# An expert layer behind attention: rows scattered to their experts' places and loaded as plain stretches, the gate kept in the table, and the first two network steps in one fixed order

## The chip, the core and the metric

One core of a Trainium2 chip runs the whole kernel in one launch. Its engines work beside each other, each in the order of its own queue: TensorE (PE; its weight loads are listed as PEld), VectorE (DVE), ScalarE (ACT), GpSimd (POOL) and SyncE (SP), which here only issues DMAs. The metric is the time of one execution on the device in microseconds, the median of the runs. The profile is that of one such execution.

## The reference

Three layers, one behind the other; r, k and v are [4, 8, 768, 48].

```python
for t in range(768):                       # attention with a decaying state
    y[:, :, t] = r_t @ (state + (u * k_t) v_t^T)
    state = w * state + k_t v_t^T
x = y as [3072 tokens, 384]
h = x @ w_in                               # [384, 2048]
x = (h - tanh(h)) @ w_out                  # [2048, 384]
logits = normalized(x) @ normalized(expert_emb).T / tau      # 8 experts
e = argmax(logits); gate = softmax(logits)[e]
out[token] = gate * (relu(x[token] @ w1[e]) @ w2[e])         # w1 [8, 384, 1024], w2 [8, 1024, 384]
```

Each token goes to one expert, so the rows have to be sorted by expert on the device before the last layer.

## The kernel before

Tokens are worked in 24 attention tiles of 128 and in 8 blocks of 384 (TB = 3 tiles). Every product of the two networks is three matmuls, since each factor is held as a high and a low part (`hi`, `lo`; `ghi`, `glo`).

**Start.** Up to line 1276 the order is written by hand (`tc.manual_schedule`): the first three attention tiles, the conversion of the first weights (`convert`, L255 to L261 on VectorE, then `split`, L268 on ScalarE and L269 on GpSimd) and their attention states. Behind `startup.close()` (L1277) a planner with a timeline model orders the instructions of each engine; `tc.issue_after(x)` is a lower bound that the program sets for it. The steps of the first network come from the loop at L1340: one step is `ffn1` (nine matmuls into `ph`, L547), `squares` (L599, L600), `small_tanh` (L608 to L615) and, some steps later, `ffn2` (nine matmuls into `acc`, L562). Steps 0 and 1 belong to this planned part, so do the state products of the first tiles (L466, added to the state by L477) and the conversions behind the first. `IDLE` puts fillers (L538) ahead of some steps; `fill` writes them to a bank that the step overwrites. All accumulators are PSUM tiles of one pool of eight banks.

**Attention of later tiles** (`attn_tile`, L489) runs ahead of the network by about a block: GpSimd does the decays (L346, L349), the bonus (`rk`, L383, L384, two buffers under the tag "xr") and the masks (`am`, L402); VectorE puts the scores into them (L419); then TensorE multiplies (L445).

**Routing** (`finish`, L636) is a generator with a stop after each part, one per block: ScalarE copies the rows out of PSUM (`xr`, L651, two buffers), SyncE stores them to `xs` in the order of the tokens (L653); VectorE finds the best expert as a one-hot matrix (`oh`, L666), TensorE counts with it (`pk`, L671), VectorE casts each token's place (`irow`, L686); GpSimd scatters the token numbers to `tab` at those places (L697); norms, exponent and gate follow, and SyncE stores the gate behind the row in `xs` (L720).

**Experts.** They are worked in an order found on the device. `order_first` (L736) runs one block ahead of the end and names the first two. For each expert `places` (L810) reads its piece of the table (`gts`), `rows` (L818) gathers its rows from `xs` by an indirect DMA on GpSimd (L798), three tiles of 128 and, for the first three experts, a fourth that is called the overflow tile here; `load_expert` (L828) loads and converts its weights (L840, L843, L851, L852); `wide` (L894) turns the rows (`columns`, L874 to L878) and does eight steps (L547, relu L629 and L631, L562); `put` (L881) scales by the gate (L883) and scatters to `out` (L803). For the first expert the three tiles are gathered, turned and its first step multiplied while the last block is still in the first network (`COL0`); its fourth tile has to wait for the last block's routing (L1458 to L1462).

Of the kernel before, what the change touches and what calls it, by code (L numbers as in the profile page):

```python
# [29 lines left out]
def rwkv__then__tanh_ffn__then__top1_moe_kernel(  # L30
# [46 lines left out]
    NEARLY = 1  # L77
    NNAR = 2
    COL0 = (13, 15)
# [3 lines left out]
    ISTORE = 14  # L83
    FA = 6
# [6 lines left out]
    lastg = None  # L91
# [8 lines left out]
    xs = dram.tile([NT, RW], F32, name="xs")  # L100
    xd = dram.tile([NT, 2 * DM], F32, name="xd")
# [134 lines left out]
    def convert(t, dst_hi, dst_lo, win_chunk=False, by_f=False):  # L236
# [13 lines left out]
        def ops():  # L250

            for l, h in cuts:
                x = ps.tile([P, 512], I32, tag="p", name="bits")
                x = x[:, :TOK].rearrange("p (k d) -> p k d", d=P) if by_f else x[:, :l.shape[1]]
                nc.vector.tensor_scalar(out=x, in0=h, scalar1=3, scalar2=0x3FFFFFFF,  # L255
                                        op0=ALU.logical_shift_left, op1=ALU.bitwise_and)
                yield
                nc.vector.scalar_tensor_tensor(out=x, in0=l, scalar=29, in1=x,
                                               op0=ALU.logical_shift_right, op1=ALU.bitwise_or)
                yield  # L260
                mark["cut"] = nc.vector.scalar_tensor_tensor(out=l, in0=h, scalar=-0x40000000, in1=x,  # L261
                                                             op0=ALU.bitwise_and, op1=ALU.bitwise_or).ins
                yield
# [332 lines left out]
    def squares(ph):  # L596
        z = work.tile([P, TOK], F32, name="z")
        q = work.tile([P, TOK], F32, name="q")
        nc.scalar.activation(out=z, in_=ph, func=AF.Square)  # L599
        nc.scalar.activation(out=q, in_=z, func=AF.Square, scale=SS, bias=sb_t)  # L600
        return z, q
# [34 lines left out]
    def finish(j, acc, part=None):  # L636
        l = work.tile([P, TB, E], F32, name="l")
        ssq = work.tile([P, TB], F32, name="ssq")
        gw = work.tile([P, TB, 2], F32, name="gw")
# [6 lines left out]
        for t in range(TB):  # L646
            if part is not None:
                xr = part[:, t, :DM]
            else:
                xr = work.tile([P, DM], F32, name="xr")  # L650
                nc.scalar.activation(out=xr, in_=acc[t][:, :DM], func=AF.Copy)  # L651
            n = TB * j + t
            nc.sync.dma_start(out=xs[n * P:n * P + P, :DM], in_=xr)  # L653
# [40 lines left out]
        root = None  # L694
# [841 lines left out]
```

## Time and profile before

| | |
|---|---|
| runs | 781.63, 781.47, 778.47 us; median 781.47 |
| the profiled execution | 780.2 us, of which the span from first to last instruction 778.6 |
| PE busy | 761.0 us (98%), 6157 matmuls; mean granted clock 0.991 |
| DVE, ACT, POOL busy | 481.3, 454.9, 300.5 us |
| chain that ended last, by engine | PE 87%, ACT 3%, DMA 3%, issue 3%, the rest 4% |
| DMA | 87.36 MB, mean 112 GB/s |

The page gives busy times over the whole span. With TensorE busy nearly throughout, the page itself tells little of where time can be won; the list of what each engine waited for and the table of stretches (windows) tell more. A window's row gives, for each engine, its busy time within the stretch and the number of its instructions, then TensorE's granted clock as a share of full speed, the share of the DMA engines that moved data, and the rate.

### The profile page before, as it was taken

What the parts mean: (1) busy time and instruction counts of PE and PEld (TensorE: products, weight loads), DVE (VectorE), ACT (ScalarE), POOL (GpSimd) and SP (SyncE); (2) the same over time, 40 slices, a digit from 0 to 9 for tenths busy, and PEclk for the clock granted to TensorE, in tenths of its full rate; (3) what the DMA queues carried; (4) which work ended last, traced back from release to release, by engine and by line L of the source; (5) the groups of instructions that cost most, each with busy time, mean ns of one, the idle gap of its engine ahead of it and who ended that gap; (6) DMA issues with size and microseconds to landing.
All of it is one profiled execution on the core that took longest, in us unless ns stands there. A gap on an engine that the chain in (4) does not pass through costs nothing.

```text
span 778.6 us, 16001 instructions
## 1 busy us (share of the span) xinstructions
PE 761.0 (98%) x6157; PEld 723.0 (93%) x6157; DVE 481.3 (62%) x1076; ACT 454.9 (58%) x1054; POOL 300.5 (39%) x319
## 2 busy tenths in 40 slices
PE   9899999999999999999999999999899999999996
PEld 5689899999999999999999999998889999999996
DVE  7967975786666755765755754756564445545430
ACT  5687776665656557556656666777253445544431
POOL 3743670564641750850751540132431124312311
PEclk9899999999999999999999999999999999999999
DMA  8934350344231330330232201160463345545500
GB/s 273 302 101 140 116 182 22 93 133 130 60 119 60 87 121 21 91 131 25 90 87 91 89 2 62 32 191 32 120 217 92 114 152 184 170 145 172 179 30 31
DMA packets 41831, 87.36 MB, mean 112 GB/s; under 512 B 9718, under 2 KB 21424, under 8 KB 40722
## 3 DMA queue, kind: packets, MB, share of 16 engines
q1 hardware_dynamic: 37042, 76.74, 31.3%
q0 software_dynamic: 4288, 9.51, 3.8%
q8 instruction: 50, 0.82, 0.5%
q14 instruction: 35, 0.29, 0.1%
q10 hardware_dynamic: 416, 0.00, 0.0%
HBM read 67.38 MB, written 19.40 MB: 111 GB/s over the span
## 4 chain that ended last, share of the span: by engine, by line
PE 87%; ACT 3%; issue 3%; DMA 3%; DVE 1%; SPq 1%; POOL 1%; POOLq 0%; DVEq 0%; ACTq 0%
PE acc L562 37%; PE ph L547 36%; PE py L445 5%; PE pa L414 3%; DMA eraw<-in_moe_w_dram 1%; PE pt L874 1%; DMA ktab<-xs,gts 1%; PE warm L154 1%; PE pst L466 1%; SPq L720 1%; PE ph L958 1%; PE ph L538 1%; PE accn L562 1%; ACT wq L851 1%; PE pl L294 0%
## 5 line engine op out<-in xcount | busy, mean ns | idle before, releaser
L547 PE MATMUL ph<-xt,wq 128*128 128x384 f32 (+4 forms) x1712 | 337.4, 340 | 2.1 <-ACT wt L286 1.3
L547 PEld LDWEIGHTS ph<-xt,wq 128*128 128x128 f32 x1712 | 300.5, 188 | 6.2 <-ACT wt L286 1.5
L562 PE MATMUL acc<-wq,ghi 128*128 128x392 f32 (+2 forms) x1120 | 289.0, 344 | 0.1
L562 PEld LDWEIGHTS acc<-wq,ghi 128*128 128x128 f32 (+1 forms) x1120 | 200.6, 187 | 5.0 <-issue 1.0
L562 PE MATMUL acc<-wq,glo 128*128 128x392 f32 (+2 forms) x552 | 182.7, 341 | 0.0
L599 ACT ACTIVATE z<-ph 128x384 f32<-128x384 f32 x128 | 62.6, 489 | 89.1 <-PE ph L547 88.6
L608 DVE TENSOR_TENSOR ph<-ph,z 128x384 f32<-128x384 f32 x128 | 71.8, 561 | 51.9 <-ACT z L599 51.2
L562 PEld LDWEIGHTS acc<-wq,glo 128*128 128x128 f32 (+1 forms) x552 | 103.0, 188 | 0.3
L610 ACT ACTIVATE ghi<-ph 128x384 fp32r<-128x384 f32 x128 | 62.8, 490 | 60.2 <-DVE ph L609 56.2
L615 DVE TENSOR_TENSOR glo<-ph,ghi 128x384 fp32r<-128x384 f32 x128 | 70.8, 553 | 42.6 <-ACT ghi L610 42.5
L803 POOL DMA_INDIRECT out_dram<-ob,gts x27 | 27.9, 1034 | 153.6 <-ACT ob L883 148.4
L600 ACT ACTIVATE q<-z,sb_t 128x384 f32<-128x384 f32 x128 | 78.9, 617 | 3.5
L609 DVE SCALAR_TENSOR_TENSOR ph<-q,ph 128x384 f32<-128x384 f32 x128 | 71.8, 561 | 11.8 <-ACT q L600 3.5
L612 ACT ACTIVATE mk<-z,lz_t 128x384 bf16<-128x384 f32 x128 | 77.2, 603 | 0.0
L631 DVE SCALAR_TENSOR_TENSOR glo<-ph,ghi 128x384 fp32r<-128x384 f32 (+2 forms) x56 | 30.7, 548 | 64.5 <-ACT ghi L629 64.5
L629 ACT ACTIVATE ghi<-ph 128x384 fp32r<-128x384 f32 (+4 forms) x56 | 27.4, 489 | 67.3 <-PE ph L547 67.3
L852 DVE TENSOR_TENSOR wq<-eraw,wq 128x768 fp32r<-128x768 f32 x60 | 55.3, 961 | 15.8 <-ACT wq L851 15.2
L851 ACT ACTIVATE wq<-eraw 128x768 fp32r<-128x768 f32 x64 | 50.5, 837 | 9.8 <-DMA eraw<-in_moe_w_dram 9.6
L383 POOL TENSOR_TENSOR rk<-rkv 128x384 f32<-128x384 f32 x18 | 18.4, 1021 | 91.4 <-ACT xr L651 49.6
L269 POOL TENSOR_TENSOR wq<-wraw,wq 128x768 fp32r<-128x768 f32 (+1 forms) x17 | 30.7, 1806 | 43.3 <-ACT wq L268 40.4
L402 POOL TENSOR_TENSOR am<-ident,cd 128x512 f32<-128x512 f32 x36 | 36.9, 1050 | 8.9 <-DVE cd L388 8.9
L482 POOL TENSOR_TENSOR st<-st,pw 112x384 f32<-112x384 f32 x20 | 16.7, 837 | 50.7 <-DVE st L475 35.0
(289 smaller groups left out, 897.0 us busy)
## 6 DMA issues: line engine op xcount, KB each, us to landing
eraw<-in_moe_w_dram SPq DMA_DIRECT2D x32, 768.0 KB, 4.8
rkv<-in_rows_dram SPq DMA_DIRECT2D x18, 640.0 KB, 5.7
tt<-in_cols_dram SPq DMA_DIRECT2D x22, 448.0 KB, 4.6
xd<-xt SPq DMA_DIRECT2D x8, 1152.0 KB, 6.1
wraw<-in_moe_w_in_dram SPq DMA_DIRECT2D x8, 768.0 KB, 9.0
wraw<-in_moe_w_out_dram SPq DMA_DIRECT2D x8, 768.0 KB, 9.3
xs<-xr SPq DMA_DIRECT2D x21, 192.0 KB, 2.6
rkv<-in_rows_dram SPq DMA_DIRECT2D x4, 256.0 KB, 9.8
```

The source lines that it names most:

```text
L445: nc.tensor.matmul(out=self.py[32 * g:32 * g + 32, kk, :], lhsT=lhs, rhs=rhs, start=start, stop=stop)
L547: mark["ph"] = nc.tensor.matmul(out=ph, lhsT=lhs[a][:, kk, :], rhs=rhs(b, kk), start=(kk == 0 and p == 0), stop=(kk == nk - 1 and p == 2)).ins
L562: mm = nc.tensor.matmul(out=acc[t][:lhs.shape[1]], lhsT=lhs, rhs=rhs(b, i), start=(i == span[0] and p == 0), stop=(i == span[1] - 1 and p ...
L599: nc.scalar.activation(out=z, in_=ph, func=AF.Square)
L600: nc.scalar.activation(out=q, in_=z, func=AF.Square, scale=SS, bias=sb_t)
L608: nc.vector.tensor_tensor(out=ph, in0=ph, in1=z, op=ALU.mult)
L609: nc.vector.scalar_tensor_tensor(out=ph, in0=q, scalar=KC, in1=ph, op0=ALU.add, op1=ALU.mult)
L610: mark["ghi"] = nc.scalar.activation(out=ghi, in_=ph, func=AF.Copy).ins
L612: nc.scalar.activation(out=mk, in_=z, func=AF.Relu, bias=lz_t, accum_out=zx[:, step:step + 1])
L615: mark["glo"] = nc.vector.tensor_tensor(out=glo, in0=ph, in1=ghi.bitcast(F32), op=ALU.subtract).ins
L851: nc.scalar.activation(out=hi[c][:, a], in_=t[:, a], func=AF.Copy)
L852: engs[s % len(engs)].tensor_tensor(out=lo[c][:, a], in0=t[:, a], in1=hi[c][:, a].bitcast(F32), op=ALU.subtract)
```

## The change

Six things are done.

1. Rows are no longer stored in the order of the tokens. `finish` keeps the three copies (tags "x2t", "x2t", "xr") and, once the places are known, GpSimd scatters the whole rows to a new DRAM tensor `xe` at their places.
2. The gate goes as a second word into the token's entry, and `tab` is scattered behind the gate instead of ahead of the norms. `finish` has one stop more, and `FIN` names the steps of the following block at which it goes on.
3. `rows` is a plain load of a stretch of `xe` on SyncE; `places` moves to GpSimd's queue; the weights of the next expert are issued behind the row loads.
4. `clear_rows` writes zeros to the middle of each expert's region of `xe`, so that places that no token takes hold numbers.
5. Of the first expert's steps, the first is multiplied behind the last accumulation of the first network, and the next expert is begun one step later (`NEARLY`, `COL0`).
6. The product, state and conversion work of steps 0 and 1 of the first network goes into the part with the fixed order, the state addition between the two squares; the scaling of the expert embedding goes to ScalarE and its transposes to step 2.

```diff
-    NEARLY = 1
+    NEARLY = 2
-    COL0 = (13, 15)
+    COL0 = (13,)
+    FIN = (3, 4, 6, 10)
+    xe = dram.tile([E * REG + P, DM], F32, name="xe")
...
@@ finish
-                xr = work.tile([P, DM], F32, name="xr")
+                xr = work.tile([P, DM], F32, name="xr", tag="xr" if t == TB - 1 else "x2t")
                 nc.scalar.activation(out=xr, in_=acc[t][:, :DM], func=AF.Copy)
-            nc.sync.dma_start(out=xs[n * P:n * P + P, :DM], in_=xr)
+            src.append(xr)
...
-        for t in range(TB):
-            with tc.issue_after(root) if root else ExitStack():
-                apart("tab", nc.gpsimd.indirect_dma_start(
-                    out=tab, out_offset=bass.IndirectOffsetOnAxis(ap=irow[:, t:t + 1], axis=0),
-                    in_=tokid[:, TB * j + t, :], in_offset=None))
-            if j == NB - 1 and t == 0:
-                root = norms()
+        def scattered(to, t, rows):
+            ins = nc.gpsimd.indirect_dma_start(
+                out=to, out_offset=bass.IndirectOffsetOnAxis(ap=irow[:, t:t + 1], axis=0), in_=rows, in_offset=None)
+            apart("tab" if to is tab else "xe", ins)
+            return ins.ins
+
+        yield
+        for t in range(TB):
+            mark["xe"] = scattered(xe, t, src[t])
         yield
-        if j < NB - 1:
+        with tc.issue_after(mark["xe"]):
             norms()
...
-        nc.vector.tensor_copy(out=gw, in_=se[:, :, None].to_broadcast([P, TB, 2]))
+        nc.vector.tensor_copy(out=tokid[:, own, 1:2].bitcast(F32), in_=se[:, :, None])
         for t in range(TB):
-            mark["gw"] = nc.sync.dma_start(out=xs[n * P:n * P + P, DM:], in_=gw[:, t, :]).ins
+            mark["tab"] = scattered(tab, t, tokid[:, TB * j + t, :])
@@ order_first
-        for t in flat:
-            nc.gpsimd.memset(t, 0.0)
@@ rows
-            lastg = gather(g, gts[:m, jb, t], n).ins
+            mark["rows"] = nc.sync.dma_start(out=g[:, :DM], in_=xe[bass.ds(row + t * P, m), :]).ins
@@ load_expert
-            with tc.issue_after(mark["gts"]) if jb == 1 else ExitStack():
+            with tc.issue_after(mark["rows"]) if jb > 0 else ExitStack():
@@ put
-        a = nc.scalar.activation(out=ob, in_=acc, func=AF.Copy, scale=g[:, DM:DM + 1])
+        a = nc.scalar.activation(out=ob, in_=acc, func=AF.Copy, scale=gt[:, 1:2].bitcast(F32))
@@ ahead
-        if jb > 0:
-            places(jb + 1, 0, nt)
-        nxt = rows(jb + 1, 0, nt, NT)
+        nxt = rows(jb + 1, 0, nt)
+        if jb == 0:
+            places(0, TB, TB + 1)
+        places(jb + 1, 0, nt)
@@ embedding_rows, embedding_columns
-        mark["en"] = nc.vector.tensor_scalar(out=en, in0=en, scalar1=en_n, scalar2=None, op0=ALU.mult).ins
+        with tc.issue_after(mark["act"]):
+            nc.scalar.activation(out=en, in_=en, func=AF.Copy, scale=en_n)
@@ clear_rows, called at step ISTORE behind store_x
+        regions = xe[:E * REG].rearrange("(e r) d -> e r d", e=E)[:, TOK - P:TOK + P].rearrange("e (a p) d -> a p e d", p=P)
+        with tc.issue_after(mark["w"]):
+            for a in range(2):
+                nc.sync.dma_start(out=regions[a], in_=zero[:, None, :].to_broadcast([P, E, DM]))
@@ start
     embedding_rows()
+    early = [ffn1([win(p, 0) for p in range(2)], columns_of(xts[0]), NK, TOK)]
+    a[0].state_product()
+    early.append(squares(early[0], a[0].state_add))
+    convert_now(True)
+    a[TB].decay_r(nc.vector)
+    mark["pool"] = split(*ready[2])[1]
+    early.append(ffn1([win(p, 1) for p in range(2)], columns_of(xts[0]), NK, TOK))
+    a[1].state_product()
+    a[2].turned()
+    def next_rows():
+        a[1].state_add()
+        mark["act"] = a[2].turned_rows()
+    early.append(squares(early[2], next_rows))
     startup.close()
...
@@ end of the last block
+    with tc.issue_after(mark["acc"]):
+        next(wides[0])
+    for _ in range(3):
+        next(fin)
+    sl = sl + rows(0, TB, TB + 1)
     for _ in fin:
         pass
-    places(0, TB, TB + 1)
-    places(1, 0, TB + (KOV > 1))
     order_rest()
-    sl = sl + rows(0, TB, TB + 1, NT)
```

## Rows read from the trace of the kernel before

**Rows 1.** What TensorE waited for over the span: us in total, times, longest us.

```profile
PE pt L874 <- DMA ktab<-xs,gts: 2.9, 1, 2.9
PE pk L671 <- DVE oh L666: 1.5, 1, 1.5
...
PE pa L414 <- POOL wq L269: 1.3, 1, 1.3
```

**Rows 2.** Windows round the hand-over: PE, PEld, DVE, ACT, POOL; clock, DMA, GB/s.

```profile
540.20:541.70 1.50, 0.07 (x1) 0.00 (x0) 1.36 (x9) 1.46 (x5) 0.00 (x0) 1.00 0.06 22
541.70:559.50 17.80, 17.76 (x108) 17.45 (x108) 8.72 (x52) 4.21 (x11) 7.41 (x9) 1.00 0.33 87
559.50:562.40 2.90, 0.05 (x1) 0.05 (x1) 1.14 (x2) 1.58 (x2) 2.51 (x3) 1.00 1.05 397
562.40:567.50 5.10, 5.10 (x25) 5.00 (x26) 4.79 (x12) 3.33 (x6) 0.30 (x1) 0.67 0.71 202
```

**Rows 3.** Chain that ended last, 536 to 584 us: start, us, what.

```profile
548.15 3.50 SPq L720
...
555.51 6.79 DMA ktab<-xs,gts
...
569.16 1.58 PE ph L547 x9
```

**Rows 4.** Timeline of GpSimd at the hand-over: start, us, instruction [idle before].

```profile
543.42 1.03 POOL L697 DMA_INDIRECT tab<-tokid,irow  x1 [6.74 <-DVE key L773]
...
546.96 0.96 POOL L697 DMA_INDIRECT tab<-tokid,irow  x1 [0.30 <-issue]
```

**Rows 5.** Timeline of VectorE at the hand-over.

```profile
542.97 0.17 DVE L686 CAST irow<-row 128x3 int32<-128x3 f32 x1
```

**Rows 6.** DMA issues: out<-in, queue, count, KB each, median us to landing.

```profile
xs<-xr SPq DMA_DIRECT2D x21, 192.0 KB, 2.6
```

**Rows 7.** The output's scatters, line 803, from 500 us on: ns least/median/most; landing.

```profile
L803 POOL DMA_INDIRECT out_dram<-ob,gts x27: 923/1016/1401, 575.0 to 773.5; - x27
...
DMA to landing us min/median/max: 2.5/3.0/5.9
```

**Rows 8.** Windows of the start.

```profile
21.40:27.20 5.80, 5.65 (x57) 4.58 (x57) 5.73 (x16) 2.52 (x6) 3.77 (x5) 1.00 1.05 288
27.20:30.20 3.00, 1.09 (x9) 0.97 (x8) 3.00 (x7) 2.90 (x10) 3.00 (x2) 1.00 1.03 373
30.20:37.30 7.10, 6.45 (x32) 4.72 (x33) 7.10 (x13) 6.63 (x19) 6.82 (x5) 0.56 0.85 255
```

**Rows 9.** Timeline of ScalarE at the start.

```profile
25.99 0.94 ACT L268 ACTIVATE wq<-wraw 128x768 fp32r<-128x768 f32 x1 [2.24 <-DVE wraw L261]
26.81 0.50 ACT L599 ACTIVATE z<-ph 128x384 f32<-128x384 f32 x1
27.18 0.66 ACT L477 ACTIVATE st<-pst 48x192 f32<-48x192 f32 x2
27.86 0.61 ACT L600 ACTIVATE q<-z,sb_t 128x384 f32<-128x384 f32 x1
```

**Rows 10.** Timeline of TensorE at the start.

```profile
35.74 2.08 PE L538 MATMUL ph<-ones 128*128 128x384 bf16 x6 [0.47 <-ACT ktok L360]
```

**Rows 11.** Timelines of GpSimd, VectorE and TensorE in one block of the first network.

```profile
249.84 1.02 POOL L383 TENSOR_TENSOR rk<-rkv 128x384 f32<-128x384 f32 x1 [20.15 <-DMA xs<-xr]
...
256.26 2.05 POOL L402 TENSOR_TENSOR am<-ident,cd 128x512 f32<-128x512 f32 x2
...
259.82 1.33 DVE L419 COPY_PREDICATED am<-cmask,pa 128x512 f32<-128x512 uint8 x2
...
264.43 0.42 PE L445 MATMUL py<-tt,st 112*32 112x128 f32 x8
```

**Rows 12.** Timeline of SyncE behind the start.

```profile
108.29 0.94 SPq L525 DMA_DIRECT2D xd<-xt  x2
137.03 0.34 SPq L324 DMA_DIRECT2D tt<-in_cols_dram  x1
```

More of the change, by code (lines that the diff above doesn't have):

```diff
@@ L90, in rwkv__then__tanh_ffn__then__top1_moe_kernel @@
     wides = {}
-    lastg = None
     final = None
@@ L250, in ops @@
         def ops():
[L252 to L262, printed above, removed]
+            bits = {}
+            for n, s in sorted(((n, s) for n in range(2) for s in range(3)), key=lambda x: x[::-1] if abreast else x):
+                l, h = cuts[n]
+                if s == 0:
+                    x = ps.tile([P, 512], I32, tag="p", name="bits")
+                    x = x[:, :TOK].rearrange("p (k d) -> p k d", d=P) if by_f else x[:, :l.shape[1]]
+                    bits[n] = x
+                    nc.vector.tensor_scalar(out=x, in0=h, scalar1=3, scalar2=0x3FFFFFFF,
+                                            op0=ALU.logical_shift_left, op1=ALU.bitwise_and)
+                elif s == 1:
+                    nc.vector.scalar_tensor_tensor(out=bits[n], in0=l, scalar=29, in1=bits[n],
+                                                   op0=ALU.logical_shift_right, op1=ALU.bitwise_or)
+                else:
+                    mark["cut"] = nc.vector.scalar_tensor_tensor(out=l, in0=h, scalar=-0x40000000, in1=bits[n],
+                                                                 op0=ALU.bitwise_and, op1=ALU.bitwise_or).ins
                 yield
@@ L638, in finish @@
         ssq = work.tile([P, TB], F32, name="ssq")
-        gw = work.tile([P, TB, 2], F32, name="gw")
+        src = []
         for t in range(TB):
@@ L810, in places, with rows @@
     def places(jb, t0, t1):
-        with tc.issue_after(lastg) if jb > 1 else tc.issue_after(mark["gw"]):
-            eng = nc.gpsimd if jb > 1 else nc.sync
-            row = eng.value_load(sxi[0:1, jb, 0:1], min_val=0, max_val=(E - 1) * REG)
-            mark["gts"] = eng.dma_start(out=gts[:, jb, t0:t1], in_=tab[bass.ds(row + t0 * P, (t1 - t0) * P), :]
-                                        .rearrange("(t p) b -> p t b", p=P)).ins
-    def rows(jb, t0, t1, n):
-        nonlocal lastg
+        row = nc.gpsimd.value_load(sxi[0:1, jb, 0:1], min_val=0, max_val=(E - 1) * REG)
+        nc.gpsimd.dma_start(out=gts[:, jb, t0:t1], in_=tab[bass.ds(row + t0 * P, (t1 - t0) * P), :]
+                            .rearrange("(t p) b -> p t b", p=P))
+    def rows(jb, t0, t1):
+        row = nc.sync.value_load(sxi[0:1, jb, 0:1], min_val=0, max_val=(E - 1) * REG)
         res = []
@@ L1331, in step2 @@
             accs[j] = [ps.tile([P, DL], F32, tag="p", name=f"acc{t}") for t in range(TB)]
-        ffn2(i, spans[j], g, wout, accs[j])
+        mark["acc"] = ffn2(i, spans[j], g, wout, accs[j])
     third = attention(2)
@@ L1448, in rwkv__then__tanh_ffn__then__top1_moe_kernel @@
             if j == NB - 1 and i in (8, 9, 12, 15):
-                next(ld, None)
+                with tc.issue_after(mark["ghi"]) if i == 15 else ExitStack():
+                    next(ld, None)
             if j == NB - 1 and i in COL0:
@@ L1483, in rwkv__then__tanh_ffn__then__top1_moe_kernel @@
             nc.gpsimd.dma_start(out=gt, in_=tab[bass.ds(row, P), :])
-            gather(xo[0], gt, NT)
+            nc.gpsimd.dma_start(out=xo[0][:, :DM], in_=xe[bass.ds(row, P), :])
             for _ in narrow(0, (gt, xo[0])):
```

60 lines of the change are left out of this document (28 added, 32 removed).

## The prediction

> **What bounds the kernel now.** I read the busy lines of the page first (table above): TensorE is busy 761.0 of 778.6 us, so only what stands between its instructions, and the stretches in which its clock is low, can be won. Next the list of TensorE's waits [rows 1], then the windows round the two places where they lie [rows 2, 8], then what each wait hangs on [rows 3 to 5, 9, 10]. The reader is to see that from 100 to 540 us TensorE waits for nothing, so the attention and the first network pay only if this change hurts them, and that the change touches both places that do pay.
>
> Place one is the hand-over from the first network to the experts. TensorE stands 1.46 us for the one-hot matrix of the last block, then has 17.8 us of work, then stands 2.86 us for the fourth tile of rows of the first expert, and after this second stop its granted clock is 0.67 on average for 5.1 us, part of it at 1.2 instead of 2.4 GHz [rows 1, 2]. The chain to that tile is long: SyncE writes the rows, the gate stores hold SyncE's queue for 3.50 us, the table is read, and the indirect gather takes 6.79 us from issue to use, since the first expert weights were issued just ahead of it [rows 3].
>
> Place two is the start, 21 to 37 us. VectorE is full there (5.73 of 5.80, 3.00 of 3.00, 7.10 of 7.10 us), TensorE has 1.09 us of work in the middle 3.00, and in the 7.10 us behind it its clock is 0.56 [rows 8]. ScalarE is full as well behind 27.2 (2.90 of 3.00, 6.63 of 7.10), and at 35.74 six fillers, with the third step's matmuls behind them, wait for its copy L360 [rows 8, 10].
>
> **The change, part by part.** The sum is made against the profiled execution, 780.2 us with a span of 778.6; the median of the runs is 781.47, 1.27 higher.
>
> *One product step put behind the last accumulation* (COL0, and the wide step behind mark "acc"). The nine matmuls of the first expert's first step are 1.58 us [rows 3]. Before, they ran ahead of the last accumulation; now they stand between it and the one-hot product. All before that comes 1.6 us sooner, and the 1.46 us stop is filled. VectorE gets one more relu (L631) among the routing operations, ScalarE one more copy; half a microsecond each, so I take 1.4 of 1.46, bounds 0.8 and 1.5.
>
> *The fourth tile.* Removed: three row stores, three gate stores on SyncE, the table read and the indirect gather as links of its chain. Added: three indirect scatters of whole rows to xe, then one plain load. In the old time less 1.6: the places are cast at 543.14 [rows 5], so 541.5; the first scatter goes at 541.8 and three of 1.0 with 0.3 between end at 545.7 [rows 4]. The nearest scatter of rows of this width is that of the output, 2.5, 3.0 or 5.9 us from issue to landing (least, median, most) [rows 7], so the last one, issued at 544.5, lands at 547.5, at the latest at 550.4. The load of 192 KB is bounded by the row store of the same size, 2.6 us [rows 6], and by the old gather, 6.79 [rows 3]: the tile is there at 550, with the worst of both at 557.2. TensorE, which ends the one-hot product near 540.1 and still has the 17.8 us of [rows 2], asks at 557.9. The stop of 2.86 us goes whole, with 0.7 to 8 us to spare; I go by the nearest rows, median and 2.6. I take 2.9; bounds 1.5 and 2.9, the lower if the weights collide with the load as they did before.
>
> *The clock behind it.* 5.1 us at 0.67 lose 5.1 x 0.33 = 1.7 us [rows 2]; the fall comes only behind the stop. I take 1.6, bounds 0 and 1.7. What is late next: the short stop of the overflow tile's product for L961 stays, and the conversions of the second expert's weights, which used to fall into the stop, now run beside a busy TensorE. VectorE is busy 4.79 of 5.1 us there [rows 2], but a step is used two steps later, so I count 0.3 against it, up to 1.5.
>
> *Norms, gates and table later.* The gate is needed first when an output is copied, behind all eight steps of the first expert; that work hides it, at no cost. Without that cover it would be three table scatters at 1.0 with gaps of 0.3 [rows 4], 4 us. The table is read on GpSimd's queue behind those scatters; the first output scatters queue behind the read and have the same cover.
>
> *Rows and weights of the later experts on SyncE.* TensorE does not wait there now (none of [rows 1] lies there): 0. SyncE loses 24 row and 24 gate stores.
>
> *Clearing part of xe.* Two stores on SyncE of 128 x 8 x 384 x 4 bytes, 3.1 MB together. They go on SyncE's queue behind the stores of x that are issued at 108.3; its next load is at 137.0 [rows 12]. At the 202 to 397 GB/s of [rows 2] they take 8 to 16 us. That gap hides it: 0. Without it, a load would be late by as much, and a tile of attention with it.
>
> *Row scatters in the seven earlier blocks.* Three more per block on GpSimd, 1.0 and 0.3 us each: 4.0 us. The narrowest place of the block that I followed has 4.8 us of room: GpSimd's masks end at 258.3 and the product that uses them starts at 264.4, with 1.33 us of VectorE between [rows 11]. GpSimd also loses a wait: it stood 20.15 us there for the old row stores to free a buffer [rows 11]. I take 0, bounds 0 and the rival below.
>
> *The first two steps in a fixed order.* ScalarE idled 2.24 us ahead of the conversion at 25.99, and z, the two state copies and q (0.50 + 0.66 + 0.61 = 1.77 us) came behind it [rows 9]; the first step's product that they follow stands at the head of the first window of [rows 8]. Written ahead of it, they leave a chain that is full down to 35.74: 1.8 us. The scaling of the expert rows moves from VectorE to ScalarE, as one copy: nearest is the 0.5 of [rows 9], so minus 0.5. The fillers took 2.08 us at the low clock [rows 10], half at the full one: plus 1.0. Sum 2.3. Upper bound: from 27.2 to 37.3 TensorE did 1.09 + 6.45 x 0.56 = 4.7 us of work at full clock in 10.1, so 5.4. Lower bound: VectorE is full in all three windows and loses almost nothing, so 0, and minus 2 if the new order stalls an engine that the planner had filled.
>
> On the clock there, what the rows show is single short waits, 1.3 us the longest [rows 1], and a clock of 0.56 behind them. The Trainium skill ("TensorE: Matmul & The Clock Gate", section on psum-queue depth-cycling) says that cycling through the PSUM banks makes TensorE idle in bits, often enough that the clock swings between its two levels. By that rule the fall would stay even when the longest wait is gone, and the start would be worth 1.3, not 2.3. No row decides it; the waiting for banks (L360 frees one) speaks for it, the 1.09 of 3.00 us against.
>
> Sum: 1.4 + 2.9 + 1.6 - 0.3 + 2.3 = 7.9. From 780.2 that is 772.3, from the median 773.6; I say **773.0**.
>
> **The rivals.** *Only the hand-over pays.* The start stays bound by VectorE, full in [rows 8], and its clock low: gain 5.6 to 6.6, time 774 to 776.5. For it: VectorE's windows; against: what TensorE waits for at 35.74 is a copy of ScalarE.
>
> *The wait changes its place.* The tile comes behind the weights, with the worst landing of [rows 7] and the 6.79 of [rows 3] and another 1 us, or the conversions hold the relus. Then 1.5 to 4 us of the hand-over are lost, clock and all: gain 4 to 6.4 with the start as forecast, 1.6 to 4 without: 775 to 780. Against it: 8 us of spare by the nearest rows.
>
> *Slower: GpSimd sets the pace of attention.* Its queue is in order, and a row scatter holds what stands behind it until the places are known. With 4.0 us of scatters and w us of waiting per block against 4.8 us of room, attention is late by w - 0.8, seven times. It cancels the gain at w = 0.8 + 7.9/7 = 1.9 us; at w = 3 it costs 15.4 us: 780.2 - 7.9 + 15.4 = 788. For it: the room is small. Against it: the 20 us stop that goes away, and each scatter is written two steps behind its places. Output scatters lasted 0.92 to 1.40 us each beside a working VectorE [rows 7]. The Trainium skill ("SBUF — State Buffer", section Who interferes with whom) says that a VectorE instruction in a two-port mode blocks GpSimd's descriptor writing for its whole length; by that rule more scatters mean more of the 1.40 kind, 0.4 x 3 = 1.2 us of w per block, which still falls short of 1.9.
>
> *It does not do what it says.* The planner may place the product step elsewhere, and the 1.46 us stop stays: within the second rival's range.
>
> **How the numbers follow.** Forecast (both places pay, 770.5 to 775.5): 0.53. Only the hand-over, 774 to 776.5: 0.18. The wait changes its place, 775 to 780: 0.15. The start at its upper bound, 3 us better than forecast, 769 to 771: 0.06. Slower by GpSimd: 0.05; a stalled start of minus 2 with a poor hand-over, 779 to 782: 0.03. The range leaves out the last two cases and the far end of the third: 768.5 to 778.5. A measurement of this kernel can tell about 0.5% from no change, 3.9 us. Faster by more, below 777.6: 0.53 + 0.18 + 0.04 + 0.06 = 0.81; within: 0.11 + 0.03 = 0.14; slower by more: 0.05.
>
> **What would show it.** TensorE's waits after the change: no stop over 0.5 us for the one-hot matrix or a tile of rows, and a granted clock of 1.0 for the 20 us behind. The fourth tile's load on SyncE lands near 551 in the old time. The third step's matmuls start before 36 us instead of behind the fillers of [rows 10]. No TensorE stop between 100 and 530; if one shows, the attention rival holds. The prediction fails if the load waits for the weights, or if TensorE at 25 to 40 us is as slow as before.

## The result, and the profile after

The changed kernel takes 786.71 us (median of 6 runs, 784.79 to 790.61); beside it the kernel before took 780.19 (778.47 to 781.63). The ratio is 1.009 with a 95% interval of 1.0061 to 1.0119: slower by nearly 1%, where 773.0 was forecast and 778.5 was the end of the range. The profiled execution took 787.1 us, with a span of 785.5 against 778.6.

First the list of TensorE's waits (us in total, times, longest us). Both stops of the hand-over in [rows 1] are gone, the one for the one-hot matrix and the one for the tile of rows. A longer one stands in their place (the first line below), two new ones of 2 us elsewhere, and two short ones in the last block:

```profile
PE acc L567 <- ACT ghi L636: 5.4, 1, 5.4
PE pt L289 <- ACT ktok L365: 2.1, 1, 2.1
PE pst L471 <- issue: 2.0, 5, 0.5
...
PE acc L567 <- ACT ghi L617: 0.7, 1, 0.7
PE acc L567 <- DVE glo L622: 0.5, 1, 0.5
```

Windows round the hand-over, columns as in [rows 2]: 22.3 us without a gap, then 5.4 us of nothing, then 5.9 us at a granted clock of 0.61, so most of it at 1.2 instead of 2.4 GHz.

```profile
543.40:565.70 22.30, 22.30 (x139) 21.73 (x138) 10.38 (x62) 5.95 (x16) 7.69 (x11) 1.00 0.46 98
565.70:571.10 5.40, 0.00 (x0) 0.00 (x0) 2.95 (x4) 3.57 (x6) 2.35 (x4) 0.79 0.51 168
571.10:577.00 5.90, 5.89 (x22) 5.33 (x23) 3.95 (x14) 1.81 (x5) 3.50 (x5) 0.61 0.95 280
```

What TensorE waits for is read from the timelines of GpSimd, SyncE, ScalarE and TensorE, in that order (start, us, instruction, [idle before]):

```profile
550.71 0.96 POOL L701 DMA_INDIRECT xe<-xr,irow  x1 [0.31 <-issue]
...
555.68 1.04 POOL L701 DMA_INDIRECT tab<-tokid,irow  x1 [2.71 <-DVE exc L1005]
...
568.72 5.88 POOL L814 DMA_DIRECT2D gts<-tab  x8 [9.47 <-DMA tab<-tokid,irow]
```

```profile
554.47 0.35 SPq L823 DMA_DIRECT2D ktab<-xe  x1
555.01 1.51 SPq L823 DMA_DIRECT2D rkv<-xe  x3
556.74 0.59 SPq L823 DMA_DIRECT2D u_bc<-xe  x1
557.95 1.05 SPq L839 DMA_DIRECT2D eraw<-in_moe_w_dram  x2
```

```profile
566.98 1.58 ACT L850 ACTIVATE wq<-eraw 128x768 fp32r<-128x768 f32 x2 [8.31 <-DMA eraw<-in_moe_w_dram]
569.10 1.58 ACT L850 ACTIVATE wq<-eraw 128x768 fp32r<-128x768 f32 x2 [0.54 <-DMA eraw<-in_moe_w_dram]
570.59 0.47 ACT L636 ACTIVATE ghi<-ph 128x384 fp32r<-128x384 f32 x1
```

```profile
571.11 2.29 PE L567 MATMUL acc<-wq,ghi 128*128 128x384 f32 x6 [5.41 <-ACT ghi L636]
```

SyncE's queue works in order. All row loads need the last row scatter, so it stands until 554.47; the second expert's weights are written behind five of these loads and go out at 557.95. The first of them land near 567, 9 us after their issue. ScalarE works in order too: the relu of the first expert's seventh step stands behind four conversions of these weights, and TensorE behind the relu.

The same order stood in the kernel before. Its one-hot product, its first conversions of these weights and that relu were:

```profile
541.73 0.18 PE L671 MATMUL pk<-oh,tri 128*128 128x8 bf16 x1 [1.46 <-DVE oh L666]
...
560.38 1.58 ACT L851 ACTIVATE wq<-eraw 128x768 fp32r<-128x768 f32 x2 [5.01 <-DMA eraw<-in_moe_w_dram]
...
563.97 0.47 ACT L629 ACTIVATE ghi<-ph 128x384 fp32r<-128x384 f32 x1
```

There the weights went out at 554.76 and landed 5.6 us later. The one-hot product came 3.3 us earlier too, so times are best counted from it: the weights' issue is at 13.0 us before and 12.9 after, hence not later; their landing is at 18.7 before and 22.0 after; the relu is done at 22.7 before and 26.0 after. TensorE asks for it at 20.7 in the changed kernel. Before, the stop for the tile of rows, from 17.8 to 20.6, put this asking off behind 22.7, so the wait did not show.

To see where the rest went, the span is cut at four TensorE instructions that every kernel has: the last product of the logits (pl), the one-hot product of the sixth block, that of the last block (pk), and the count after the first expert (pok). For the profiled run of after they are:

```profile
126.69 0.63 PE L299 MATMUL pl<-wt,ent 128*32 128x128 f32 x12
439.83 0.18 PE L677 MATMUL pk<-oh,tri 128*128 128x8 bf16 x1
545.02 0.18 PE L677 MATMUL pk<-oh,tri 128*128 128x8 bf16 x1
587.05 0.18 PE L1036 MATMUL pok<-ok,ones 128*128 128x8 bf16 x1
```

The differences, in us, here and in the experiments' traces (each one execution; names as below). Where the hand-over is written alike, two executions still differ by 2.6 us (before and new_start) and by 3.4 (wf_ghi and wf_ghi_again), so a smaller difference in that column is weak evidence by itself; the changed kernel's three executions lie at 42.0 to 43.0:

| kernel | to pl | to 6th pk | to last pk | to pok | to end |
|---|---|---|---|---|---|
| before | 128.97 | 307.33 | 105.43 | 38.50 | 198.4 |
| forecast change | -2.3 | 0 | -1.4 | -4.2 | 0 |
| after, as profiled | 126.69 | 313.14 | 105.19 | 42.03 | 198.4 |
| after_again | 128.89 | 307.31 | 106.27 | 42.98 | 198.4 |
| after_same | 127.13 | 312.70 | 105.86 | 41.98 | 198.3 |
| weights_first | 129.44 | 307.31 | 104.75 | 34.93 | 198.5 |
| wf_ghi | 128.82 | 307.32 | 103.71 | 35.26 | 198.4 |
| wf_ghi_again | 126.87 | 307.32 | 103.56 | 38.68 | 198.5 |
| wf_ghi_tab | 127.22 | 309.88 | 104.16 | 36.53 | 198.4 |
| weights_mid | 126.73 | 312.59 | 104.01 | 42.60 | 198.5 |
| no_tab | 126.80 | 307.32 | 105.38 | 41.18 | 198.3 |
| tab_late | 129.30 | 307.32 | 105.60 | 39.21 | 198.4 |
| tab_late_same | 128.06 | 311.20 | 105.88 | 40.45 | 198.3 |
| new_start | 130.19 | 307.50 | 105.35 | 35.94 | 198.3 |
| before_wf | 131.01 | 307.30 | 105.53 | 34.60 | 198.5 |
| product_behind | 129.48 | 307.37 | 104.97 | 36.70 | 198.4 |

So the later experts are as they were, and three stretches went otherwise than forecast: the hand-over (last pk to pok), the last block ahead of it, and, in some executions, the first block. In the profiled run they make the 6.9 us of the two spans: -2.3 at the start, +5.8 in the first block, -0.2 in the last, +3.5 in the hand-over.

### The profile page after: what moved, and what is told of

Its sections match the earlier page's. It is cut to its first block, busy times and chain, and to the rows that moved or that the text cites. A ratio compares the mean times of both kernels' runs of the same rounds, so it can differ in the third digit from the quotient of the medians.

```text
span 785.5 us, 16012 instructions
## 1 busy us (share of the span) xinstructions
PE 762.3 (97%) x6157; PEld 723.4 (92%) x6157; DVE 481.3 (61%) x1075; ACT 454.8 (58%) x1055; POOL 293.1 (37%) x312
## 4 chain that ended last, share of the span: by engine, by line
PE 84%; DMA 5%; issue 4%; ACT 2%; DVE 2%; POOL 1%; SPq 1%; POOLq 0%; DVEq 0%; ACTq 0%
PE acc L567 36%; PE ph L552 35%; PE py L450 5%; PE pa L419 3%; DMA eraw<-in_moe_w_dram 3%; PE pt L873 1%; PE pst L471 1%; DMA xe<-xr,irow 1%; DMA rkv<-xe 1%; ACT wq L850 1%; PE accn L567 1%; SPq L823 0%; POOL out_dram L804 0%; PE pt L289 0%; DVE bits L263 0%
## 5 line engine op out<-in xcount | busy, mean ns | idle before, releaser
L851 DVE TENSOR_TENSOR wq<-eraw,wq 128x768 fp32r<-128x768 f32 x60 | 54.9, 956 | 19.2 <-ACT wq L850 18.7
L701 POOL DMA_INDIRECT tab<-tokid,irow x24 | 23.8, 992 | 36.5 <-DVE tokid L726 28.8
L701 POOL DMA_INDIRECT xe<-xr,irow x21 | 20.7, 987 | 40.1 <-issue 31.2
```

Of the source, the lines that this page charges most:

```text
L701: ins = nc.gpsimd.indirect_dma_start(out=to, out_offset=bass.IndirectOffsetOnAxis(ap=irow[:, t:t + 1], axis=0), in_=rows, in_offset=None)
L851: engs[s % len(engs)].tensor_tensor(out=lo[c][:, a], in0=t[:, a], in1=hi[c][:, a].bitcast(F32), op=ALU.subtract)
```

## The experiments

Ratios are to the kernel before beside it on the same chip; its median lay between 778.8 and 780.2. Each kernel starts from the changed one unless it says otherwise.

**weights_first.** SyncE loads the second expert's first two pieces of weights ahead of all these rows.

```diff
+    ld1 = load_expert(1, sxi[0:1, 1, 1:2], gate0)   # its two first loads
+    next(ld1)
     sl = sl + rows(0, TB, TB + 1)
...
```

> The changed kernel with one move: SyncE issues the first two loads of the second expert's weights ahead of the load of the fourth tile of rows and of the second expert's rows, not behind them. Theory A (weights that come late, on a ScalarE that works in order: the loads stood on SyncE behind row loads that had to wait for the row scatters, the conversions waited 8.3 us, and the relu of the next step stood behind them): the loads go out near 545 us instead of 557.95, the conversions wait for nothing, TensorE's stop of 5.4 us and the low clock behind it go, and the kernel takes 778 to 782 us, against 786.7 of the changed kernel. Theory B (the row scatters themselves make the hand-over longer, in whatever order the loads stand): the weights now share the DMA engines with the scatters, the fourth tile lands later than its 560 us by as much as the weights gain, and the time stays at 785 us or more.

776.38 us, ratio 0.9965 (0.9948 to 0.9982): theory A, and below its 778. That is 12.5 thousandths below the changed kernel as first run and 9.3 below after_again, whose trace lacks the gaps of the last section: some 7 us for the move itself. From pk to pok it takes 34.93 us, 7.1 less than the changed kernel; the last of the two loads goes out at 540.30. What TensorE waits for from 500 to 600 us:

```profile
PE pt L975 <- ACT hh L972: 1.6, 2, 0.9
PE acc L569 <- DVE glo L624: 0.5, 1, 0.5
PE acc L569 <- ACT ghi L619: 0.3, 1, 0.3
```

**conv_behind.** The conversions stand behind the relus instead (their generator is advanced from step 6 on, `if i >= 6 if jb == 0 else ...`).

> The changed kernel with one move: the conversions of the second expert's first two pieces of weights are issued behind the relus of the first expert's last two steps, not ahead of them. The loads stay where they are, late. Theory A1 (only the order on ScalarE costs, the late weights alone would be covered): the stop of 5.4 us for the relu goes, and the time is 779 to 783 us. Theory A2 (the late weights cost wherever the conversions stand): the stop moves to the first product of the second expert, which now waits for the conversions, and the time stays within 2 us of the 786.7 of the changed kernel.

781.14 us, 1.0033 (1.0015 to 1.0052). By the time A1, by the trace A2: the 5.4 us stop is gone, but late weights now hold up what stands behind them on ScalarE and VectorE: 3.0 us for hh of the fourth tile's own product, and 2.9 of the next step for xn, a copy of that tile. Its profiled run was no faster in the hand-over (42.75 us). The order on ScalarE alone is not the cause.

**weights_mid.** The weights between the fourth tile's load and the second expert's rows.

> The changed kernel with the second expert's first two weight loads on SyncE between the fourth tile of rows and the second expert's rows: ahead of four loads (672 KB), but still behind the wait for the row scatters. It tells apart why the weights of the changed kernel landed near 569 us, 11 us after their issue. Waiting theory (the loads stand behind the scatters' end at 554.5): issue moves from 557.95 to about 555 and the landing by those 3 us only, so the relu still stands behind the conversions for 2 to 3 us: 780 to 783 us. Sharing theory (the four row loads ahead of them took the DMA engines): issue at 555, landing 5.5 us after it as in the kernel before, near 560.5, so the conversions end before the relu is due: 776 to 778 us.

785.87 us, 1.0079 (1.0059 to 1.0098): worse than both theories, with the gaps of the last section in its trace. The weights went out at 554.88, yet landed 7.6 us later, and now the rows behind them were late:

```profile
PE pt L885 <- DMA rkv<-xe: 5.6, 1, 5.6
```

Neither the place on the queue nor the four row loads explain that. The DMA queues of after do (packets, MB, share of the 16 engines' time), from 559 to 564 us and then from 564 to 569; q1 carries SyncE's loads, q0 GpSimd's scatters:

```profile
q1 hardware_dynamic: 135, 0.26, 86.1%
q0 software_dynamic: 21, 0.00, 0.4%
```

```profile
q1 hardware_dynamic: 678, 1.32, 70.5%
q0 software_dynamic: 32, 0.00, 0.5%
```

In the first stretch (5 us of 16 engines) a packet of the loads, some 2 KB, took 5 x 16 x 0.861 / 135 = 0.51 us of an engine, in the second 0.083. What was on its way in the first were the three table scatters (8 bytes a row), issued 555.7 to 558.3; GpSimd's next step waits for them until 568.7, 9.5 us (in the kernel before they went out between 543.4 and 547.0 [rows 4], ahead of these loads, and landed 3.1 to 5.4 us after their issue). The change had moved them behind the gates, into the middle of these loads. Two kernels try that.

**no_tab** leaves out the last block's table scatters; **tab_late** leaves nothing out, and holds them behind the conversions by placing the copy of the gates there on VectorE (what is left of `fin`); the two reads of the table follow them.

```diff
+            if jb == 0 and i == 5:
+                with tc.issue_after(mark["conv"]):
+                    for _ in fin:
+                        pass
+                places(0, TB, TB + 1)
+                places(1, 0, TB + (KOV > 1))
...
```

> The changed kernel without the last block's three table scatters (left out: the last block's tokens get no place in the table, so their rows are not put back; the table's loads for the last part no longer wait and go out earlier). Order and loads on SyncE are those of the changed kernel. Collision theory (the table's 8-byte writes hold up every load that is on its way beside them): the weights, issued near 556 us, land 5.5 us later instead of 10.5, TensorE's stop of 5.4 us shrinks to under 1, and the time falls by 4 to 6 us, to 778 to 781 us on a chip where the changed kernel takes 784. Queue theory (the weights are late because they stand behind the row loads): the landing stays near 10 us, the stop at 5, the time at 783 to 786.

> The changed kernel with nothing left out, its last table scatters held until the second expert's first two pieces of weights are converted (the copy of the gates into the table's rows stands behind these conversions on VectorE). Collision theory: as without the scatters, weights 5.5 us after issue, no stop of 5 us, 778 to 781 us. Queue theory: no difference, 783 to 786 us. Rival for a loss: the loads of the table's entries, 8 bytes each too, now come later and the first expert's last tile waits for its gate: 786 or more.

780.59 us, 1.0019 (1.0005 to 1.0032), and 778.81 us, 0.9995 (0.9981 to 1.0009). The trace of tab_late from 559 to 564 us, its conversions, and its stop:

```profile
q1 hardware_dynamic: 626, 1.22, 64.6%
```

```profile
561.95 1.58 ACT L852 ACTIVATE wq<-eraw 128x768 fp32r<-128x768 f32 x2 [6.07 <-DMA eraw<-in_moe_w_dram]
```

```profile
PE acc L567 <- ACT ghi L636: 3.0, 1, 3.0
```

Packets are back at 0.083 us (5 x 16 x 0.646 / 626), the weights land 5.9 us after their issue at 556.04, and the stop is 3.0 instead of 5.4. The collision theory holds for the packets. no_tab met it less well: packets took at most 0.10 us, but the landing was 7.2 us after the issue and the stop 4.1, not under 1. It is not a clean test, since the 8-byte reads of the table no longer wait there and run beside the weights.

**after_same, tab_late_same.** Both once more, on one chip.

> The changed kernel as it is, for the size of the next one's difference on one chip: 783.5 to 787 us, a stop of 5.2 to 5.6 us for the relu behind the late conversions.

> The changed kernel with its last table scatters held behind the conversions of the second expert's first two pieces of weights, beside the changed kernel on one chip. In the traces so far its stop is 3.0 us instead of 5.4 and the stretch from the routing's product to the end of the first expert is 39.2 us instead of 42.0 to 43.0: 3 to 4 us less than the changed kernel. If the medians of the earlier calls hold (778.8 against 783.7 to 786.7), 5 us or more: then something besides this stop goes too.

788.11 us, 1.0118 (1.0095 to 1.0142), over its expectation, and 783.40, 1.0047 (1.0030 to 1.0064): the table scatters' place is worth 4.7 us there. The profiled pair shows 2.1 of it in the spans (786.0 and 783.9), 1.5 of that in the hand-over (stop 4.9, under its expectation, and 3.3); the rest of the 4.7 is not located.

Counted from each trace's one-hot product, in us, the stop follows the landing, and the issue hardly moves:

| kernel | weights issued | first landed | relu done | TensorE asks | stop |
|---|---|---|---|---|---|
| before | 13.0 | 18.7 | 22.7 | behind the tile | none |
| after | 12.9 | 22.0 | 26.0 | 20.7 | 5.4 |
| after_again | 12.8 | 22.3 | 26.2 | 20.7 | 5.6 |
| after_same | 13.7 | 21.9 | 25.6 | 20.7 | 4.9 |
| no_tab | 13.5 | 20.7 | 24.8 | 20.7 | 4.1 |
| tab_late_same | 13.5 | 20.0 | 24.0 | 20.7 | 3.3 |
| tab_late | 13.8 | 19.7 | 23.7 | 20.7 | 3.0 |

With the landing of the kernel before, the stop would still be 22.7 - 20.7 = 2.0 us (an estimate from the first two rows). An earlier issue, as in weights_first, takes it away whole.

**after_again.** The changed kernel on another chip.

> The changed kernel as it is, beside the others of this call. In its profiled run the first block's state products stood in gaps at 152 to 156 us (2.0 us) with the clock at 0.91 in that stretch, and 3.8 us were lost there; three other kernels with the same row scatters show no such gaps. If the gaps belong to the change they are here again. If they belong to that one execution, the stretch is without gaps, and the profiled run is near 783 to 785 us of span, with the stop of about 5.3 us for the relu as before. Median 785 to 787 us.

783.66 us, 1.0058 (1.0038 to 1.0078). Below its expectation, and no gaps in the state products: with the same instruction order they come in some executions only, see the last section.

**old_start, wf_old_start, new_start.** The first two steps as before, in the changed kernel and in weights_first; and the new start alone in the kernel before.

> The changed kernel with the start of the kernel before: its last part, the first two steps in one fixed order, is undone. My prediction had this part worth 2.3 us (from 2 us lost to 5.4 gained). Read from the trace of after it is worth 1.0 us at 54 us of the span: then this kernel takes 787 to 789 us. Theory C (the new start is paid back later, by about 4 us between 140 and 160 us where the state products stood in gaps): undoing it gives 782 to 785 us and the gaps are gone. If the gaps come from the row scatters, they are still there with the old start.

> The changed kernel with the second expert's weights loaded ahead of the rows and with the start of the kernel before. Two readings of the start: at the last product of the first logits, near 129 us, three kernels with the new start stand at 126.7, 129.4 and 128.9 us and three with the old one at 129.0, 129.7 and 129.5, so the new start is worth about 1 us: then this kernel takes 777 to 778 us, against 776.4 with the new start. Or what the new start gains comes back as low clock later (each of its three traces has one stretch more at 0.91): then there is no difference, or this kernel is faster, 774 to 776 us.

> The kernel before with the new start alone (the first two steps in one fixed order, the two halves of a conversion abreast). The prediction's term: 2.3 us gained, 776.5 us. From the traces so far (five kernels with the new start stand at 126.7 to 129.4 us at the last product of the first logits, mean 128.6, five with the old one at 129.0 to 131.0, mean 129.7): about 1.2 us, 777.6. Rival from the pair of the changed kernel with and without it: nothing, 778.8. The low clock near 30 us stays in each case.

784.71 us, 1.0068 (1.0049 to 1.0086); 778.57, 0.9995 (0.9982 to 1.0008); 778.62, 0.9988 (0.9974 to 1.0001). In the first the gaps are gone, as theory C says, but after_again has none either with the new start, and the start makes no difference within the intervals; in the second it makes 0.0030 or 2.3 us, in the third 0.9 us, not clear of noise. To pl, 14 traces with the new start need 126.4 to 130.2 us (mean 128.0), 6 with the old one 129.0 to 131.0 (mean 129.8): worth 1.9 us, though these are different kernels on several chips.

**product_behind.** The kernel before with the product step behind the last accumulation (`COL0 = (13,)`, and the step after mark "acc").

> The kernel before with one edit of the change alone: the product step of the first expert that stood ahead of the last accumulation is held behind it, beside the routing's vector work. The prediction's first term: the stop of 1.5 us for the one-hot goes and nothing else moves, 780.2 becomes 778.7 (778 to 779.5). Rival: TensorE only reaches the same later waits earlier, since the tile of rows and the weights land when they did: no difference, 780.

778.43 us, 0.9989 (0.9974 to 1.0003), which does not tell its two expectations apart. The stop for the one-hot matrix is gone, but two others (0.7 us) for a step's activation have come: TensorE, with one step less to do, reaches it sooner.

```profile
PE pt L874 <- DMA ktab<-xs,gts: 2.7, 1, 2.7
PE acc L562 <- ACT ghi L610: 0.7, 2, 0.5
```

**before_wf, before_orders.** The kernel before with the weights moved alone; then also with the product step and with the conversions of later pieces behind their step's activation.

> The kernel before with the move of the weights alone: the first two loads of the second expert's weights go out ahead of the routing's row and gate stores. If the move by itself brings what it brought in the changed kernel (10 us there), the late weights bounded the kernel before too, and it comes to 774 to 776 us. If TensorE's stop there was for the fourth tile of rows, as its trace says (2.9 us, tile at 562.3, while the conversions ended at 564), that stop stays and the time is 778 to 780 us: no difference.

> The kernel before with three moves in order and nothing else of the change: the second expert's weights ahead of the routing's stores, the product step behind the last accumulation, and the conversions of the first expert's later pieces behind the activation of their step. It asks how much of what the changed kernel gains when its orders are mended (774.2) comes from scattering rows to their places, and how much was to be had without. If the scatters and plain loads bring nothing by themselves: 774.5 to 776 us. If they are worth the 2.9 us of the tile and the clock behind it: 777 us or more, with a stop for the fourth tile in the trace.

776.84 us, 0.9972 (0.9960 to 0.9985), between the two expectations: the stop for the tile shrinks from 2.9 to 0.3 us, since with early conversions TensorE has 20.4 instead of 17.8 us of work ahead of that tile. So part of what the change wanted was to be had by one moved load. With all three moves 778.75, 1.0002 (0.9986 to 1.0018): TensorE comes sooner and the tile's stop is back at 2.0 us. There the old chain bounds; with rows scattered to their places it doesn't, as the next kernels show.

**wf_ghi, wf_ghi_again.** weights_first, with the conversions of the first expert's third piece behind the activation of their step.

```diff
...
-                with tc.issue_after(mark["ghi"]) if i == 15 else ExitStack():
+                with tc.issue_after(mark["ghi"]) if i >= 12 else ExitStack():
...
```

> The changed kernel with the weights loaded ahead of the rows, and with the conversions of the first expert's third piece of weights held behind the activation of their step in the last block. Its trace without this edit has two stops there, 0.30 us for the activation on ScalarE and 0.46 for the difference on VectorE behind it, at 522 us. If ScalarE's order causes them, they go: 775.5 to 776 us, against 776.4. Rival: the two moved conversions now stand in front of a later activation, and the stops only change their place: 776 to 777.5.

> The fastest so far, unchanged, beside the others on this chip: 774 to 775 us if the trace shows no gaps in the first block's state products near 152 us, 776 to 778 if it does (three executions that came 2.3 us earlier to 127 us had them and lost 5 us there, the run of wf_hh among them).

774.20 us, 0.9930 (0.9912 to 0.9948), and 774.28, 0.9940 (0.9924 to 0.9956): the fastest here, faster than both kernels, and more than the 0.8 us that its stops were. In the trace of wf_ghi TensorE is busy 59.97 of 60.00 from 500 to 560 us, and the clock stays whole to 580:

```profile
500.00:560.00 60.00, 59.97 (x356) 59.22 (x355) 42.16 (x139) 41.39 (x95) 22.04 (x21) 1.00 0.46 137
560.00:580.00 20.00, 18.09 (x98) 16.16 (x98) 10.36 (x28) 7.99 (x14) 9.00 (x11) 1.00 0.64 183
```

In that of wf_ghi_again the clock from 560 to 580 us is 0.83 and the hand-over takes 38.68 us instead of 35.26: this fall, too, is in some executions only.

**wf_hh, wf_ghi_tab.** The same with the last piece's conversions behind hh, and with the table scatters held.

> The fastest so far (weights ahead of the rows, conversions of the third piece behind their step) with one more move of the same kind: the conversions of the second expert's last piece behind the activation that the fourth tile's product waits for (a stop of 1.2 us of the two for that activation, 1.9 together). If ScalarE's order causes it, 0.9 to 1.2 us go: 773 to 773.5 us, against 774.2. Rival: the conversions end later and the second expert's own accumulation waits for them: 774 to 775.

> The fastest so far (weights ahead of the rows, conversions of the third piece behind their step) with the table scatters held in the same way. There the scatters ran beside the second expert's rows and the second half of its weights; what is left to gain is the stop of 1.2 us for an activation behind late conversions. Collision theory: 0 to 1.5 us better than the same kernel without the move. Rival: the third expert's rows and the table's loads now meet instead, no difference or up to 1 us worse.

777.19 us, 0.9986 (0.9968 to 1.0005), outside its expectation, but with the gaps of the last section in its profiled run (313.26 us to the 6th pk), so it decides nothing. 776.12, 0.9964 (0.9952 to 0.9976): 1.8 us worse than wf_ghi_again beside it. Its trace doesn't put this down to the hand-over, which is 2.2 us shorter than that of wf_ghi_again, in spite of 2.5 us for hh behind late conversions. It loses 2.6 us in the first block, which its edit does not touch, with a stop of TensorE that no other trace has:

```profile
PE ph L554 <- DVE glo L624: 1.9, 1, 1.9
```

So whether holding the scatters helps where the weights are early stays open.

## Why the prediction was wrong

*The step that failed is the sentence on the conversions that "now run beside a busy TensorE", taken at "0.3 against it, up to 1.5", together with "Norms, gates and table later ... at no cost".* The first term measured 5.4 us of stop and a clock of 0.61 for 5.9 us behind it, 2.3 us more. Its reason was that VectorE's work is used two steps later; what TensorE stood for was ScalarE's relu behind the conversions, and the conversions' input. Some 2.0 us of it could be read from the trace before: the relu was done 22.7 us behind the one-hot product, and with the tile's stop gone TensorE asks at 20.7. The other 3.3 are the weights' later landing (22.0 instead of 18.7). The table's step asked who waits for what is moved, and found nobody, rightly: the table was read by 574.6 us, and the first output scatter waited for its copy until 581.7. It did not ask what the moved writes run beside. tab_late, which moves them away again, has 2.4 us less stop.

*"Rows and weights of the later experts on SyncE"*, taken at 0, is the step that left a gain lying. The weights' issue is not later than before, but they wait for nothing and stand behind row loads that wait for the scatters. With the weights loaded ahead of these, the hand-over is 7.1 us shorter (weights_first).

The rival with "the conversions hold the relus" is what happened, but it ended where the whole gain of the hand-over is lost; the hand-over lost the forecast 4.2 and 3.5 to 4.5 more. Its size should have come from the conversion's last input, not from the spare of the tile.

Of the 14.8 us between the forecast for the profiled run (772.3) and its 787.1, the hand-over makes 7.7, the gaps in the first block 5.8, the last block 1.2. For the gaps the prediction had no term, and their cause stays open. Without them, in after_again, the changed kernel takes 783.66 us: still outside the range, by the hand-over and the last block.

The Trainium skill ("DMA: Bandwidth & Descriptors", section Issuing engines are not separate DMA queues) says that transfers run on the same 16 engines and interleave, whichever engine issued them. The rows above agree, and put a size to it: SyncE's packets six times as long beside GpSimd's 8-byte writes. The same page (Specifications) has transfers below 512 bytes done as read-modify-write; no run here shows whether that is why.

*The fourth tile* went as forecast. The last scatter landed 9.4 us behind the one-hot product (forecast 7.4), and TensorE, asking 17.6 us behind it, did not wait.

*The product step.* 1.4 forecast; alone it brought 0.4 us (product_behind), not clear of noise: its trace has TensorE run into the activation it used to reach later, and the changed kernel's has 1.2 us of such stops. With that order mended the stretch to the last pk is 1.7 us shorter (wf_ghi): right in mechanism, with a cover that was not seen.

*The clock behind the tile.* 1.6 forecast from one execution. In new_start, which has the hand-over of the kernel before, with a stop of 1.8 us for the tile, the clock from 560 to 580 us was 1.00 instead of 0.91 and the stretch to pok 35.94 instead of 38.50; in product_behind, with a stop of 2.7, it was 1.00 and 36.70. The fall is not in every execution, so the term holds part of the time only.

*The start.* 2.3 forecast, 1.9 in the mean of the traces, from -1.2 to 2.5 against before. The third step's matmuls start at 35.65 us, as the prediction's sign has it, instead of 37.37. But where the fillers stood TensorE now waits 2.1 us for ScalarE's copy `ktok`, 0.5 before. The clock from 20 to 40 us was 0.83 to 0.91 with the new start and 0.74 to 0.83 with the old one: the fall stays. That agrees with the Trainium skill's rule on psum-queue depth-cycling ("TensorE: Matmul & The Clock Gate"); no run shows that this cycling causes it, since with the 2.1 us a long wait is still there.

*Row scatters in seven blocks*, *clearing xe* and *later experts* cost 0 as forecast: 307.1 to 307.5 us to the 6th pk with and without them. GpSimd does not set the pace of attention. The exceptions are the gaps below and wf_ghi_tab.

Taken together, wf_ghi has what the prediction saw, with its orders mended: 4.6 to 5.0 us gained, of 7.9.

## What to carry to other kernels

Before a stop is counted as won, look for what would hold the engine next, and count both from the same event: here the next wait stood in the trace before, hidden by the stop. When a store or a load is moved off a critical path, list what it now stands ahead of on its in-order queue and which transfers are on their way beside it; "nobody waits for it" is half the question. A load that waits for nothing belongs ahead of loads that wait. A small gain from filling a stop should be tried together with the next activation in line, since TensorE arrives there sooner.

## What was not expected of the hardware

Some 384 writes of 8 bytes (three scatters) made the 2 KB packets of other loads take 0.51 us of a DMA engine instead of 0.083, for some 4 us. It is not this execution alone: in the slowest 2 us between issue and landing of the weights they took 0.27 to 0.82 us in the six kernels that have these writes beside them (after, after_again, after_same, conv_behind, old_start, weights_mid), and 0.10 to 0.13 in no_tab, tab_late_same and tab_late. Whether it is their size or their being scattered isn't shown.

A VectorE instruction on three numbers per partition (`rn`, the norms behind the row scatters, in the first block) took 0.50 us in after, 3.28 in wf_ghi_again and 6.18 in wf_ghi_tab, there from 156.34 to 162.52, while GpSimd ran six instructions of 0.8 to 1.3 us one behind the other until 162.49. In the kernel before, the longest of its eight was 1.01. VectorE's next step had to wait, and in wf_ghi_tab TensorE with it: the stop of 1.9 us above.

In five of thirteen traces with both the row scatters and the new start (after, after_same, weights_mid, wf_hh, tab_late_same), and in none of the seven others, TensorE's state products of the first block stand in groups of five or six, with waits that nothing in the trace ends:

```profile
153.17 0.31 PE L471 MATMUL pst<-rkv,ktok 128*32 128x48 f32 x6 [0.48 <-issue]
153.94 0.29 PE L471 MATMUL pst<-rkv,ktok 128*16 128x48 f32 x5 [0.46 <-issue]
154.68 0.30 PE L471 MATMUL pst<-rkv,ktok 128*32 128x48 f32 x6 [0.45 <-issue]
```

With the low clock behind them (0.66 for 5 us in four of the five, 1.00 in tab_late_same) they cost 3.9 to 5.9 us of the stretch to the 6th pk. The changed kernel's three medians, each on another chip, go with it: 786.7 and 788.1 where its trace has the gaps, 783.7 where it hasn't. The row scatters' transfers are on their way at that time, but also in traces without gaps; the cause stays open.
